# Key products from ScalarE to VectorE, state decay from ScalarE to GpSimd, and two regrouped slots, in a fused attention, FFN and MoE kernel

## Chip, cores and metric

The kernel runs on 1 core of one Trainium2 chip. The metric is the device time of one execution in microseconds (us), the median of several runs. All times here are in us unless marked ns.

## The reference, cut to what matters

Three stages follow each other on 2 x 768 = 1536 tokens of width 512 (8 heads of 64): a linear attention with decay, a dense FFN, and a mixture of experts with one expert per token.

```python
# 1 attention, per batch and head, in blocks, kv_state starts at 0
intra = einsum(einsum(qb, kb) * Dmask, vb)          # Dmask = lam ** (i - j), i >= j
inter = einsum(qb * lam_pow, kv_state)
out   = intra + inter
kv_state = lam_block * kv_state + einsum(kb * rev_pow, vb)
# 2 dense FFN: w_in 512 x 2048, w_out 2048 x 512
h = x @ w_in;  x2 = maximum(0.01 * h, h) @ w_out
# 3 MoE, 8 experts of 512 x 1024 x 512
logits = x2 @ w_gate + modality_bias[modality_id];  e = argmax(logits)
out = softmax(logits)[e] * (maximum(x2 @ w1[e], 0) @ w2[e])
...
```

## The kernel before, in words

The order of all instructions is written by hand: each engine runs its own instructions in the order in which the program emits them, and waits for semaphores of the others where it needs their data or a free buffer. So an instruction that waits holds up everything that was emitted behind it on its engine.

**Attention.** Each batch is cut into 6 chunks of 128 tokens, 12 chunks in all, taken in the order of the list ORD: (0,0), (1,0), (0,1), (1,1), (0,2), (1,2), (0,3), (0,4), (0,5), (1,3), (1,4), (1,5), as (batch, chunk). Chunk n goes through these steps:

- at_scores (L290): 8 TensorE products of keys and queries into two PSUM banks.
- at_prep_q (L276, VectorE): the queries times powers of lam, in place.
- at_mask (L304, VectorE): two products of 128x512, scores times the decay mask.
- at_prep_k (L282): the keys times each head's factor for their token, in place, needed only for the state. Before, it is 8 ScalarE instructions of 128x64 (one per head, L288), often emitted in two halves of 4 heads.
- at_out (L317): 8 to 16 products into one bank (masked scores times values, then state times queries), and xt_split (L341), which rounds the result on ScalarE (xh, L349) and takes the rest on VectorE (xl, L350). Chunks 4 and 5 are first copied by ScalarE (L337) and split later.
- at_state (L352): 8 small products of keys and values, and the decay of the state tile in place. Before, the decay is 4 ScalarE instructions of 128x128 (L368) for each chunk whose number within its batch is 1 to 4.
- at_state_add (L372): VectorE adds the products to the state (two instructions of 64x256, L382).

**FFN.** Two chunks make a token block j of 256 tokens (j = 0 to 5). The hidden width 2048 is cut into 16 slices f. A unit is u = 16 j + f, 96 in all. The main loop (L1499) runs iterations i over a list seq of units: blocks 0 and 1 are interleaved (0, 1, 2, 16, 3, 17, ...), from u = 32 on they are in order. One iteration emits ff1 of its unit (12 TensorE products of 128x256 into one of two banks, ScalarE's scaled copy t, L399), ff1_max (VectorE, L404), ff1_split (ScalarE gh, L411; VectorE gl, L412), then ff2 of the unit two iterations earlier (6 products of 128x512, L425), and then the hooks of its unit: attention and routing steps that a table `at(j, f, fn, ...)` has put there. In block j, slot f means unit 16 j + f.

In iterations 0 to 25 the dense weights are also converted from 64-bit floats: three VectorE bit operations per weight slice (L1485, L1490), ScalarE's rounding (L1495), VectorE's remainder (L1497). One slice has 512 KB, and one to two slices are done per iteration.

**Routing.** When block r is through the FFN, evac_x2 (L445) copies its two banks to tiles x2s, of which there is one pair, on ScalarE (L451) and VectorE (L453), and stores them to DRAM. route_dot is 16 VectorE dot products of 128x512 (8 experts, 2 tiles, L503), two per unit. route_v1 (VectorE) picks the expert, route_rk (TensorE, L535 to L539) ranks the tokens with small products, route_v2 and route_gate follow; route_gate stores the gate column of x2s to DRAM.

**Towards the experts.** In the last block (j = 5) the first expert's weights are loaded and split into a rounded part (ScalarE, L865) and a remainder (VectorE, L866): first_w1(i) and first_w2(i) for i = 0 to 3, placed in slots of that block. early_idx, first_gather and TX(0) prepare the first gathered tokens. Then come the expert products G1 and G2.

The slots that the change touches:

```python
SLOT = {2: (None, 2, 5, 7, 10, 10, 12, 13, 15)}   # others: (5, 6, 8, 8, 11, 10, 12, 13, 13)
s_ld, s_a, s_o, s_s, s_d, s_a2, s_o2, s_s2, s_d2 = ...
# load, first(n), out(n), state(n), add(n), first(n+1), out(n+1), state(n+1), add(n+1)
at(2, 10, lambda: evac_x2(1))      # banks 3, 4, where chunk 7's scores go (sb = 3, 4)
RSLOT = {..., 4: (82, 1, 89, 90)}  # first dot unit, experts per unit, route_v1, route_rk
```

Of the kernel before, what the change touches and what calls it, by code (L numbers as in the profile page):

```python
# [12 lines left out]
AF = mybir.ActivationFunctionType  # L13
# [7 lines left out]
E, FE = 8, 1024  # L21
# [18 lines left out]
def tile_attention_ffn_moe(  # L40
# [241 lines left out]
    def at_prep_k(n, heads=range(H)):  # L282
        b, c = ORD[n]
        t = chunks[n]
        if c + 1 >= NCH:
            return
        for h in heads:
            nc.scalar.activation(out=t["k"][:, h, :], in_=t["k"][:, h, :], func=AF.Copy, scale=dec[:, h, C - 1:C])  # L288
# [63 lines left out]
    def at_state(n, bk):  # L352
# [13 lines left out]
        if c > 0:  # L366
            for g in range(4):
                nc.scalar.activation(  # L368
                    out=state[b][:, g, :], in_=state[b][:, g, :], func=AF.Copy, scale=lq[:, g, C - 1:C]
                )  # L370
# [946 lines left out]
    at_mask_tw(1)  # L1317
    at_out(0, 3)
    at_out(1, 4)
    at_prep_k(0)  # L1320
    at_prep_k(1)
    conv("wi", 1, win, V)
# [41 lines left out]
    def xt_staged(n):  # L1364
# [3 lines left out]
    at(0, 7, at_prep_k, 4, range(H // 2))  # L1368
    at(0, 8, at_prep_k, 4, range(H // 2, H))
# [5 lines left out]
    at(0, 11, at_prep_k, 5, range(H // 2))  # L1375
    at(0, 12, at_prep_k, 5, range(H // 2, H))
# [13 lines left out]
        2: (None, 2, 5, 7, 10, 10, 12, 13, 15),  # L1390
    }
    for j in range(2, last):
        n = 2 * (j + 1)
        sb = (5, 6) if j % 2 else (3, 4)
        s_ld, s_a, s_o, s_s, s_d, s_a2, s_o2, s_s2, s_d2 = SLOT.get(j, (5, 6, 8, 8, 11, 10, 12, 13, 13))
# [4 lines left out]
        at(j, s_a, at_prep_k, n, range(H // 2))  # L1400
        at(j, s_a + 1, at_prep_k, n, range(H // 2, H))
# [3 lines left out]
        at(j, s_s, at_prep_k, n + 1, range(H // 2))  # L1405
        at(j, s_s + 1, at_prep_k, n + 1, range(H // 2, H))
# [7 lines left out]
    RSLOT = {0: (32, 1, 39, 41), 1: (42, 1, 49, 51), 2: (52, 1, 59, 61), 3: (66, 1, 73, 75), 4: (82, 1, 89, 90)}  # L1414
    for r, (f0, step, fv, fr) in RSLOT.items():
        for i in range(0, E, step):
            jobs = [(e, tk) for e in range(i, i + step) for tk in range(2)]
            at(0, f0 + i // step, route_dot, r, jobs)
        at(0, fv, route_v1, r)
        at(0, fr, route_rk, r, 7)  # L1420
        at(0, fr, route_v2, r)
        at(0, fr, route_pf, r)
        at(0, fr, route_gate, r)
# [29 lines left out]
    at(last, 11, early_idx)  # L1453
    at(last, 12, first_gather)
    at(last, 15, TX, 0)
    for i in range(4):
        at(last, (3, 13, 14, 15)[i], first_w1, i)
        at(last, (6, 8, 10, 12)[i], first_w2, i)
# [230 lines left out]
```

## Time and profile before

| | us |
|---|---|
| median of 3 runs (lowest, highest) | 534.59 (531.89, 535.84) |
| profiled execution, its device time | 532.42 |
| its span from first to last instruction | 530.5 |
| mean granted TensorE clock, share of full speed | 0.980 |

Busy in that span: TensorE (PE) 499.1 us, 94%; VectorE (DVE) 316.2, 60%; ScalarE (ACT) 194.8, 37%; GpSimd (POOL) 49.7, 9%. PE is busy for nearly all of the span, so the rest is in few places: what counts is where PE stands idle, which engine it then waits for, and how fast its clock is afterwards. A share over the whole span says little about an engine in one stage.

### The profile page before, as it was taken

What the parts mean: (1) busy time and instruction counts of PE and PEld (TensorE: products, weight loads), DVE (VectorE), ACT (ScalarE), POOL (GpSimd) and SP (SyncE); (2) the same over time, 40 slices, a digit from 0 to 9 for tenths busy, and PEclk for the clock granted to TensorE, in tenths of its full rate; (3) what the DMA queues carried; (4) which work ended last, traced back from release to release, by engine and by line L of the source; (5) the groups of instructions that cost most, each with busy time, mean ns of one, the idle gap of its engine ahead of it and who ended that gap; (6) DMA issues with size and microseconds to landing.
All of it is one profiled execution on the core that took longest, in us unless ns stands there. A gap on an engine that the chain in (4) does not pass through costs nothing. (4 is left out here: it accounts for less than half of the span.)

```text
span 530.5 us, 9446 instructions
## 1 busy us (share of the span) xinstructions
PE 499.1 (94%) x3485; PEld 425.7 (80%) x3485; DVE 316.2 (60%) x796; ACT 194.8 (37%) x489; POOL 49.7 (9%) x97
## 2 busy tenths in 40 slices
PE   5868999999999799999999999899999999999994
PEld 3757988686988689788988889787789987879693
DVE  5696998887577467667477647874551251513130
ACT  2456345454433332333333334354222253322221
POOL 1000000002000000000000000020140302322111
PEclk9988999999999899999999999989999999999998
DMA  8999201701801100410050008211069608274101
GB/s 257 359 407 401 103 1 34 260 2 45 278 1 41 40 2 1 139 41 1 21 138 22 2 20 279 61 42 40 7 215 400 219 22 312 78 245 157 41 2 42
DMA packets 30669, 63.43 MB, mean 120 GB/s; under 512 B 6871, under 2 KB 8799, under 8 KB 30608
## 3 DMA queue, kind: packets, MB, share of 16 engines
q1 hardware_dynamic: 28496, 56.17, 30.8%
q0 software_dynamic: 2112, 6.52, 3.6%
q8 instruction: 29, 0.48, 0.4%
q14 instruction: 32, 0.26, 0.2%
HBM read 56.35 MB, written 6.52 MB: 119 GB/s over the span
## 5 line engine op out<-in xcount | busy, mean ns | idle before, releaser
L396 PE MATMUL hp<-xh,wi 128*128 128x256 f32 x768 | 128.5, 290 | 4.9 <-ACT xh L349 2.7
L425 PE MATMUL x<-wo,gh 128*128 128x512 f32 x384 | 122.8, 402 | 1.7 <-DVE pm L309 1.7
L396 PEld LDWEIGHTS hp<-xh,wi 128*128 128x128 f32 x768 | 110.6, 194 | 14.2 <-DVE t L404 4.7
L425 PE MATMUL x<-wo,gl 128*128 128x512 f32 x192 | 76.6, 399 | 0.1
L425 PEld LDWEIGHTS x<-wo,gh 128*128 128x128 f32 x384 | 67.4, 194 | 10.2 <-issue 1.9
L411 ACT ACTIVATE gh<-t 128x256 fp32r<-128x256 f32 x96 | 40.1, 418 | 81.9 <-DVE t L404 81.9
L396 PE MATMUL hp<-xl,wi 128*128 128x256 f32 x384 | 62.5, 285 | 0.0
L404 DVE TENSOR_TENSOR t<-t,hp 128x256 f32<-128x256 f32 x96 | 40.2, 419 | 34.2 <-ACT t L399 32.9
L412 DVE TENSOR_TENSOR gl<-t,gh 128x256 fp32r<-128x256 f32 x96 | 40.7, 424 | 33.4 <-ACT gh L411 26.1
L399 ACT ACTIVATE t<-hp 128x256 f32<-128x256 f32 x96 | 36.2, 377 | 63.6 <-PE hp L396 63.2
L954 PE MATMUL hp<-xp,w1h 128*128 128x256 f32 x320 | 58.7, 284 | 0.0
L396 PEld LDWEIGHTS hp<-xl,wi 128*128 128x128 f32 x384 | 53.5, 193 | 0.4 <-DVE xl L350 0.4
L982 PE MATMUL o<-w2h,hp 128*128 128x512 f32 x160 | 52.5, 397 | 0.0
L954 PEld LDWEIGHTS hp<-xp,w1h 128*128 128x128 f32 x320 | 50.2, 192 | 2.6 <-issue 2.5
L964 DVE SCALAR_TENSOR_TENSOR hp<-hp,hp 128x256 fp32r<-128x256 f32 x40 | 16.5, 423 | 60.0 <-ACT hp L963 27.8
L425 PEld LDWEIGHTS x<-wo,gl 128*128 128x128 f32 x192 | 36.8, 192 | 11.8 <-DVE gl L412 3.6
L954 PE MATMUL hp<-xp,w1l 128*128 128x256 f32 x160 | 45.3, 283 | 0.0
L982 PEld LDWEIGHTS o<-w2h,hp 128*128 128x128 f32 x160 | 29.8, 188 | 7.0 <-issue 1.2
L982 PE MATMUL o<-w2l,hp 128*128 128x512 f32 x80 | 31.5, 393 | 0.0
L954 PEld LDWEIGHTS hp<-xp,w1l 128*128 128x128 f32 x160 | 30.7, 192 | 0.1
L963 ACT ACTIVATE hp<-hp 128x256 fp32r<-128x256 f32 x40 | 15.2, 384 | 41.2 <-PE hp L954 40.9
L503 DVE SCALAR_TENSOR_TENSOR junk<-x2s,wgr_hi 128x512 bf16<-128x512 f32 x40 | 27.5, 689 | 0.7
(248 smaller groups left out, 625.9 us busy)
## 6 DMA issues: line engine op xcount, KB each, us to landing
rawi<-in_moe_w_in_dram SPq DMA_DIRECT2D x16, 512.0 KB, 7.9
rawo<-in_moe_w_out_dram SPq DMA_DIRECT2D x16, 512.0 KB, 7.4
raw<-in_moe_w_dram SPq DMA_DIRECT2D x16, 512.0 KB, 3.9
nr<-in_moe_w_dram SPq DMA_DIRECT2D x9, 512.0 KB, 12.3
xs_d<-x2s SPq DMA_DIRECT2D x12, 256.0 KB, 4.4
nrx<-in_moe_w_dram SPq DMA_DIRECT2D x6, 512.0 KB
wgr_hi<-in_moe_w_dram SPq DMA_DIRECT2D x6, 512.0 KB, 8.6
qT<-in_q_dram SPq DMA_DIRECT2D x10, 256.0 KB, 6.7
```

What stands on the lines that cost most here:

```text
L396: nc.tensor.matmul(hp, lhsT=w[:, hl, kk, :], rhs=xx[:, kk, :], start=(n == 0), stop=(n == 11))
L399: nc.scalar.activation(out=t, in_=hp, func=AF.Copy, scale=0.01)
L404: nc.vector.tensor_max(out=t, in0=t, in1=hp)
L411: nc.scalar.activation(out=gh, in_=t, func=AF.Copy)
L412: nc.vector.tensor_sub(out=gl, in0=t, in1=gh.bitcast(F32))
L425: nc.tensor.matmul(x2[j][tk], lhsT=a[:, ts], rhs=wout[f][:, w, :], start=(f == 0 and n == 0), stop=(f == 15 and n == 2),)
L503: nc.vector.scalar_tensor_tensor(out=junk, in0=x2s[j][tk][:, 0:512], scalar=1.0, in1=wgr[e], op0=ALU.mult, op1=ALU.mult, accum_out=lgs[j][ ...
L954: nc.tensor.matmul(hp.rearrange("p (a b) -> p a b", a=2), lhsT=w1s[kk][w][:, f * 128:(f + 1) * 128], rhs=x[:, :, ks], start=(n == 0), stop ...
L963: nc.scalar.activation(out=hi, in_=hp, func=AF.Relu)
L964: nc.vector.scalar_tensor_tensor(out=lo, in0=hp, scalar=0.0, in1=hi.bitcast(F32), op0=ALU.max, op1=ALU.subtract)
L982: nc.tensor.matmul(o2[b], lhsT=hT[b, f // 4][a][fs], rhs=w[:, f % 2, :], start=(n == 0), stop=(n == 23))
```

## The change

- at_prep_k is one VectorE product of 128x512, with the factor of each head repeated by a zero step, in place of 8 ScalarE instructions. Where it was emitted in two halves, it stands where the second half stood (chunks 4, 5, 6, 8, 10) or one unit before the chunk's at_state (chunks 7 and 9).
- The decay of the state is two GpSimd products of 64x256 (the diagonal blocks; the rest of the tile is zero), in place of 4 ScalarE instructions of 128x128.
- Before the main loop, the bit operations of the second weight slice are emitted ahead of the first two at_out, and its rounding behind them.
- In block 2 the second chunk (7) moves two units later: scores, query and mask from slot 10 to 12, out from 12 to 14, state from 13 to 15; the state add of chunk 6 moves from 10 to 9. In blocks 3 and 4 the first chunk's state (with the load of the next chunk's v and k) moves from slot 8 to 9, the second chunk's state add from 13 to 14.
- Block 4's dot products are three per unit (units 82 to 87) in place of two; route_v1 moves from unit 89 to 87, route_rk, route_v2 and route_gate from 90 to 89.
- early_idx moves from unit 91 to 90; first_w1(0) from unit 83 to 88; first_w2(0 to 3) from units 86, 88, 90, 92 to 88, 89, 91, 92.

```diff
-    def at_prep_k(n, heads=range(H)):
+    def at_prep_k(n):
         b, c = ORD[n]
         t = chunks[n]
-        if c + 1 >= NCH:
-            return
-        for h in heads:
-            nc.scalar.activation(out=t["k"][:, h, :], in_=t["k"][:, h, :], func=AF.Copy, scale=dec[:, h, C - 1:C])
+        if c + 1 < NCH:
+            nc.vector.tensor_tensor(
+                out=t["k"], in0=t["k"], in1=dec[:, :, C - 1:C].to_broadcast([128, H, D]), op=ALU.mult
+            )
...
-            for g in range(4):
-                nc.scalar.activation(
-                    out=state[b][:, g, :], in_=state[b][:, g, :], func=AF.Copy, scale=lq[:, g, C - 1:C]
+            for half in range(2):
+                p0 = half * 64
+                sl = state[b][p0:p0 + 64, :, p0:p0 + 64]
+                nc.gpsimd.tensor_tensor(
+                    out=sl, in0=sl, in1=lq[p0:p0 + 64, :, C - 1:C].to_broadcast([64, 4, 64]), op=ALU.mult
                 )
...
+    first = split64([("wi", 1, win, V)])
     at_out(0, 3)
     at_out(1, 4)
+    split64_out(*first)
     at_prep_k(0)
     at_prep_k(1)
-    conv("wi", 1, win, V)
...
-    at(0, 7, at_prep_k, 4, range(H // 2))
-    at(0, 8, at_prep_k, 4, range(H // 2, H))
+    at(0, 8, at_prep_k, 4)
...
-    at(0, 11, at_prep_k, 5, range(H // 2))
-    at(0, 12, at_prep_k, 5, range(H // 2, H))
+    at(0, 12, at_prep_k, 5)
...
-        2: (None, 2, 5, 7, 10, 10, 12, 13, 15),
+        2: (None, 2, 5, 7, 9, 12, 14, 15, 15),
...
-        s_ld, s_a, s_o, s_s, s_d, s_a2, s_o2, s_s2, s_d2 = SLOT.get(j, (5, 6, 8, 8, 11, 10, 12, 13, 13))
+        s_ld, s_a, s_o, s_s, s_d, s_a2, s_o2, s_s2, s_d2 = SLOT.get(j, (5, 6, 8, 9, 11, 10, 12, 13, 14))
...
-        at(j, s_a, at_prep_k, n, range(H // 2))
-        at(j, s_a + 1, at_prep_k, n, range(H // 2, H))
+        at(j, s_a + 1, at_prep_k, n)
...
-        at(j, s_s, at_prep_k, n + 1, range(H // 2))
-        at(j, s_s + 1, at_prep_k, n + 1, range(H // 2, H))
+        at(j, s_s2 - 1, at_prep_k, n + 1)
...
-    RSLOT = {0: (32, 1, 39, 41), 1: (42, 1, 49, 51), 2: (52, 1, 59, 61), 3: (66, 1, 73, 75), 4: (82, 1, 89, 90)}
+    RSLOT = {0: (32, 2, 39, 41), 1: (42, 2, 49, 51), 2: (52, 2, 59, 61), 3: (66, 2, 73, 75), 4: (82, 3, 87, 89)}
...
-    at(last, 11, early_idx)
+    at(last, 10, early_idx)
...
-        at(last, (3, 13, 14, 15)[i], first_w1, i)
-        at(last, (6, 8, 10, 12)[i], first_w2, i)
+        at(last, (8, 13, 14, 15)[i], first_w1, i)
+        at(last, (8, 9, 11, 12)[i], first_w2, i)
```

## Rows read from the trace of the kernel before

**Rows 1.** Windows: busy us and instruction counts of each engine, granted clock, DMA.

```profile
25.00:45.00 20.00, 12.87 (x111) 10.72 (x111) 17.95 (x35) 12.38 (x36) 0.00 (x0) 0.91 1.03 405
56.00:128.00 72.00, 69.07 (x479) 57.09 (x477) 61.84 (x128) 33.19 (x86) 3.17 (x8) 1.00 0.19 62
182.00:188.00 6.00, 6.00 (x31) 5.49 (x31) 4.53 (x11) 0.38 (x1) 0.00 (x0) 0.50 0.23 87
189.00:340.00 151.00, 149.72 (x1088) 132.64 (x1087) 102.17 (x289) 52.75 (x142) 3.88 (x21) 1.00 0.21 64
345.00:348.00 3.00, 3.00 (x12) 2.61 (x11) 2.54 (x10) 1.89 (x6) 0.67 (x2) 0.51 0.03 3
```

**Rows 2.** Timeline (start, duration, instruction, idle before and releaser): two FFN units.

```profile
335.88 0.64 PE L396 MATMUL hp<-xh,wi 128*128 128x256 f32 x4
...
338.70 0.64 PE L396 MATMUL hp<-xh,wi 128*128 128x256 f32 x4
```

**Rows 3.** Timeline, the conversion stage around chunk 4's state decay.

```profile
95.62 1.26 ACT L368 ACTIVATE st<-st,lq 128x128 f32<-128x128 f32 x4
...
97.19 0.42 DVE L404 TENSOR_TENSOR t<-t,hp 128x256 f32<-128x256 f32 x1 [1.46 <-ACT t L399]
...
97.66 0.74 PE L396 MATMUL hp<-xh,wi 128*128 128x256 f32 x4 [1.03 <-DVE t L404]
...
100.39 0.42 DVE L404 TENSOR_TENSOR t<-t,hp 128x256 f32<-128x256 f32 x1 [0.30 <-ACT t L399]
```

**Rows 4.** Timeline, the conversion stage around chunk 4's key products.

```profile
87.80 1.05 ACT L288 ACTIVATE k<-k,dec_t 128x64 f32<-128x64 f32 x4
...
88.75 0.57 ACT L337 COPY kT<-ao 128x512 f32<-128x512 f32 x1
...
89.63 0.42 DVE L404 TENSOR_TENSOR t<-t,hp 128x256 f32<-128x256 f32 x1 [1.73 <-ACT t L399]
```

**Rows 5.** Timeline, the start: a weight load, its first use, a decay, the split.

```profile
15.39 0.33 SPq L163 DMA_DIRECT2D rawi<-in_moe_w_in_dram  x1
...
23.96 0.42 DVE L1485 TENSOR_SCALAR tw<-rawi 128x512 int32<-128x512 int32 x1
...
41.46 1.26 ACT L368 ACTIVATE st<-st,lq 128x128 f32<-128x128 f32 x4
...
43.24 0.69 DVE L350 TENSOR_TENSOR xl<-ao,xh 128x512 fp32r<-128x512 f32 x1 [2.01 <-ACT xh L349]
```

**Rows 6.** The page's DMA issues: count, size of one, median us to landing.

```profile
rawi<-in_moe_w_in_dram SPq DMA_DIRECT2D x16, 512.0 KB, 7.9
```

**Rows 7.** Timeline, the scores of chunk 7 and the copy before them.

```profile
181.04 0.59 ACT L451 COPY x2s<-x 128x512 f32<-128x512 f32 x1 [0.67 <-DMA xs_d<-x2s]
...
181.68 2.67 PE L296 MATMUL sc<-qT,kT 64*128 64x128 f32 x16 [3.34 <-ACT x2s L451]
```

**Rows 8.** Timeline, block 4's rank products and VectorE's queue around them.

```profile
343.83 0.41 DVE L404 TENSOR_TENSOR t<-t,hp 128x256 f32<-128x256 f32 x1
...
343.97 0.17 PE L535 MATMUL rk<-oh,tri_b 128*128 128x8 bf16 x1 [2.28 <-DVE oh L527]
...
359.81 0.41 DVE L404 TENSOR_TENSOR t<-t,hp 128x256 f32<-128x256 f32 x1
```

**Rows 9.** Groups by form: count, busy us, mean ns of one, idle before.

```profile
L280 DVE TENSOR_TENSOR qT<-qT,lq 128x512 f32<-128x512 f32 x8 | 5.5, 689 | 3.9 <-PE sc L296 3.9
L865 ACT ACTIVATE w1h<-raw 128x1024 fp32r<-128x1024 f32 x8 | 8.1, 1049 | 0.9 <-DMA raw<-in_moe_w_dram 0.5 <-ACT hp L963 0.4
L619 POOL TENSOR_TENSOR mmat<-mmat,nst 128x64 f32<-128x64 f32 x1 | 0.3, 297 | 0.1
L1263 POOL TENSOR_SCALAR nh<-nh,xgn 32x512 f32<-32x512 f32 x3 | 4.7, 1571 | 24.1 <-DVE nh L1262 24.1
```

**Rows 10.** Timeline, VectorE beside GpSimd's only other stretch of products.

```profile
123.51 0.70 POOL L239 CAST tri_b<-tri_f 128x128 bf16<-128x128 f32 x1 [121.14 <-DMA tri_f<-in_tri_dram]
...
123.97 0.78 DVE L1497 TENSOR_TENSOR wo<-tw,wo 128x512 fp32r<-128x512 f32 x1
```

More of the change, by code (lines that the diff above doesn't have):

```diff
@@ L1411, in tile_attention_ffn_moe @@
         at(j, s_d2, at_state_add, n + 1)
-    RSLOT = {0: (32, 1, 39, 41), 1: (42, 1, 49, 51), 2: (52, 1, 59, 61), 3: (66, 1, 73, 75), 4: (82, 1, 89, 90)}
[L1415 to L1418, printed above, removed]
+    RSLOT = {0: (32, 2, 39, 41), 1: (42, 2, 49, 51), 2: (52, 2, 59, 61), 3: (66, 2, 73, 75), 4: (82, 3, 87, 89)}
+    for r, (f0, n, fv, fr) in RSLOT.items():
+        jobs = [(e, tk) for e in range(E) for tk in range(2)]
+        for i in range(0, len(jobs), n):
+            at(0, f0 + i // n, route_dot, r, jobs[i:i + n])
         at(0, fv, route_v1, r)
```

## Prediction

> **What bounds the kernel now.** I read the windows by stage first, then the waits of PE, then the timeline around each. In the windows the reader is to see that PE is busy in nearly every microsecond from unit 26 on (149.72 of 151.00 us between 189 and 340) at the full 2.4 GHz, and that the earlier stages differ: between 25 and 45 us PE does 12.87 of 20.00 us while VectorE does 17.95, and between 56 and 128 us PE does 69.07 of 72.00 with VectorE at 61.84 [rows 1]. A unit that waits for nothing takes 2.82 us on PE [rows 2].
>
> In the conversion stage (iterations 4 to 25) a unit takes longer, because a loop through two engines sets the pace: VectorE's last bit operation lets ScalarE round the weight, ScalarE's copy t queues behind that rounding, and VectorE's next ff1_max waits for t. It repeats every 3.20 us (97.19 to 100.39), and VectorE waits 0.30 us in it [rows 3]. PE has 0.38 us to spare per unit, so there whatever ScalarE does between the rounding and t is on the path. From unit 26 on PE sets the pace, with two stalls that count: 3.34 us ahead of chunk 7's scores, which wait for ScalarE's copy of the bank [rows 7], and 2.28 us ahead of block 4's rank products [rows 8]. After each, PE's granted clock is at 1.2 GHz for some time: 0.50 over the whole of 182 to 188 us, 0.51 over 345 to 348 [rows 1].
>
> **The start (to iteration 4).** ScalarE's key products of chunks 0 and 1 go, so t of unit 0 comes earlier. VectorE then meets the next wait: the third weight slice. Its load is issued at 15.39 and such a load lands 7.9 us later in the median, at 23.3 us; VectorE first reads it at 23.96 without waiting [rows 5, 6]. So 0.7 us is gained (0 if it landed just before the read), and the new key products of chunks 0 and 1 on VectorE sit in the wait for that load. From there VectorE is never idle until it waits 2.01 us for chunk 3's rounding, which stands behind chunk 2's decay of 1.26 us on ScalarE [rows 5]. Chunk 2's key product adds 0.69 us to VectorE's run (the nearest row is the query product of the same shape, 689 ns [rows 9]). Sum: 0.7 - 0.69 + 1.26 = 1.3 us. Chunk 3's decay stands between rounding and t as in the next part and gives another 1.2 if PE is not then late itself; PE is at the lower clock for part of this stretch (0.91 mean [rows 1]), so half of it is likely. I take -2.0, bounds 0 and -3.5. The bit operations of the second slice move ahead of the first two splits; they fill time in which VectorE waits for the first output, and cost at most their own length of about 1.8 us if that slice landed late, which the wait for the third slice would still cover.
>
> **The conversion stage.** Chunks 4 and 5 each lose two things from the loop. The decay: VectorE waits 1.46 us for t in place of 0.30, so 1.16 us, and PE stalls 1.03 us for it [rows 3]. The second half of the key products: the copy behind them starts at 88.75 in place of 87.80, so 0.95 us; VectorE waits 1.73 us there, which leaves room for its new 0.69 us instruction [rows 4, 9]. The first halves (unit 7 and 11) stand beside VectorE's masks and are worth nothing. Sum 2 x (1.16 + 0.95) = 4.2 us. PE's own work is next late: it needs 2.82 of the 3.20 us, so a unit without attention work catches up by 0.38, and in one with outputs or scores PE is the later one and what VectorE saved there shows only some units on. With ten such units to catch up in, nearly all of it arrives. I take -4.2, bounds -2.5 and -4.5.
>
> **GpSimd's decay.** No row shows 64x256. A product of 128x64 took 297 ns, one by a scalar of 32x512 1571 [rows 9]; between them 256 columns are 0.84 us, a pair 1.7, against 1.26 on ScalarE. Nothing queues behind it that is due: the pair can start as soon as at_out has read the state, while the add comes one to four units (2.82 us each) later. The tightest is chunk 7, state and add both at unit 47, output at 46: 1.7 us against at least one unit. If an op took over 2 us, VectorE would wait there and PE behind it by the excess. The other cost is VectorE beside GpSimd. In the one place where they overlap closely a 128x512 subtraction took 0.78 us beside a cast, against 0.69 [rows 10, 9]. A pair overlaps some three VectorE instructions: 0.3 us. It counts for chunks 2 to 5, where VectorE or the loop sets the pace: 1.2 us; later VectorE has slack (102.17 of 151 us [rows 1]). Bounds 0 and the full 4 x 1.7 = 6.8.
>
> The Trainium skill (SBUF — State Buffer, Who interferes with whom) speaks against this edit: the port is an exclusive lock, and a VectorE instruction with two SBUF inputs contends with a GpSimd instruction that reads SBUF, so that the later one "fully blocks". The 0.09 us of rows 10, in an instruction that was covered by the cast for half of its time, does not agree with a full block, but the cast has one input. By the rule the upper bound above would be the price.
>
> **Scores two units later.** The copy at 181.04 waits for the store of the gate column, the end of a chain that started with block 0's rank products; the scores want its bank [rows 7]. Emitted at unit 44, they leave PE two units (5.6 us) of work that needs neither, and the copy takes 0.59 us on ScalarE, its twin on VectorE about as long as any 128x512 there (0.69 [rows 9]). The chain itself gets shorter too, since ScalarE's key products of chunk 7, which waited there for their load, move to VectorE at unit 46. So the 3.34 us go, and with them the slow clock: 182 to 188 us at 0.50 is 3 us lost [rows 1]. Together -6.4 us. What could be late next: chunk 7's output at unit 46 is now due for ff1 of unit 48, one unit and a state product later, some 3.5 us for a rounding and a subtraction of 0.7 each; VectorE's queue (scores, query, mask and two dots in unit 44) runs late by less than the one unit that the second hp bank allows. Nothing, then; bound: half of the 6.4 back. The loads of v and k that move a unit in blocks 3 and 4 are still three units (8.5 us) ahead of their use, and SP has no store queued behind them in those units; state and adds there have the same cover. Nothing.
>
> **The last rank.** The stall of 2.28 us and the slow clock (3 us at half: 1.5 lost, with its edges near 1.9) would give 4.2 us [rows 8, 1]. I don't count them. VectorE's queue is what is late: the rank waits behind route_v1, that behind the dots, and after the rank products the same queue still runs late: from 343.83 to 359.81 five ff1_max, 3.20 us a unit against PE's 2.82 [rows 8, 2]. Dots, expert picks, index work and weight splits from unit 82 to 95 are the same in number before and after; only their order changes. So the last ff1_max of the block can't come earlier than the sum of the work lets it, and PE will wait for ff1_max of units 89 and 90, about 1 us each, where it waited for the rank. One thing is lost: the splits at units 83 to 88 had ScalarE's half (1.05 us [rows 9]) beside VectorE's dots; at unit 88 there are no dots left, and VectorE waits for it, 0.7 us (1.05 less the third of a us in which ff1_split runs beside it). I take +0.5; bounds -4.2 and +1.0.
>
> **Sum.** -2.0 - 4.2 + 1.2 - 6.4 + 0.5 = -10.9 us. Against the profiled execution (532.42, span 530.5) that is 521.5; it lay 2.2 us under the median of the runs, from which it would be 523.7. I predict 523.
>
> **Rivals.** (1) *The rank's stall pays in full*: if VectorE's queue has more slack at units 88 to 95 than I count, 4.7 us more: 518. For it: PE is 94% busy overall and its stall is real; against: the pace of rows 8. (2) *The gap of chunk 7 moves*: the later output makes unit 48 wait, or the copy is still late; the stall or the slow clock comes back by half, 526. Against: VectorE's and ScalarE's low load there (4.53 and 0.38 of 6 us [rows 1]). (3) *The start gives nothing*: the third slice lands at 23.9 and the key products lengthen VectorE's run: 525. (4) *The lock*: GpSimd's pairs block VectorE for their whole time in chunks 2 to 5: 6.8 in place of 1.2, 529. The price is GpSimd's from rows 9; the mechanism is the one that the Trainium skill states (SBUF — State Buffer, Who interferes with whom). (5) *Slower*: the same blocking with a dear decay. At the price of 32x512, 1.57 us an op, four pairs cost 12.6 us, and the whole gain before contention (12.1) is gone: that is the point from which it decides. At 2.3 us an op (two inputs, one repeated) it would be 18.4 and the time 540. Against: 297 ns at 64 columns. (6) That the change doesn't do what it says would be a rank or scores that still stall where they stood; that is within (2).
>
> **How the numbers follow.** Forecast 0.50, (1) 0.17, (2) 0.13, (3) 0.08, (4) 0.08, (5) 0.04. From (1) with the start at its better bound some 516, from (4) 529; so 516 to 528.5 leaves out (5), part of (4) and a little below. A measurement of this kernel can tell about 1% (5.3 us) from no change: faster by more has the forecast, (1), (3), most of (2) and half of (4), 0.89; within 1% the rest of (2) and (4), 0.07; slower 0.04.
>
> **What would show it.** In the profile after: no ScalarE instructions at the lines of key products and decay; ten VectorE products near 0.69 us and sixteen GpSimd ones near 0.84; in the conversion stage no wait of VectorE for t above 0.8 us, and PE's stall of 1.03 gone; PE without a stall and at full clock where chunk 7's scores stood; no wait for the rank, but PE waiting for ff1_max around units 91 and 92. The prediction is wrong if GpSimd's products stretch VectorE's beyond 0.1 us each, if a stall with a slow clock reappears between units 42 and 52, or if the stretch from unit 82 to the expert products gets shorter by more than 1 us.

## The result and the profile after

| | before | after |
|---|---|---|
| median of 4 runs (lowest, highest) | 533.77 (531.89, 535.84) | 518.39 (517.50, 519.68) |
| ratio, 95% interval | | 0.9713 (0.9668 to 0.9757) |
| profiled execution, device time | 532.42 | 519.68 |
| its span | 530.5 | 517.9 |
| mean granted TensorE clock | 0.980 | 0.988 |

The change makes the kernel 15.4 us faster by the medians; 523 was predicted, with 516 to 528.5 as range. Between the spans of the two profiled executions the difference is 12.6 us; the profiled one of after was the longest of its four, that of before lay under its median.

Where it came from is read by one mark that both traces have 96 times, the start of ff1_max on VectorE. Its start before less its start after is the gain up to that iteration:

| iteration | before | after | gain | stage behind it |
|---|---|---|---|---|
| 4 | 50.99 | 47.15 | 3.84 | start |
| 14 | 85.00 | 81.17 | 3.83 | conversion, no attention work |
| 26 | 130.69 | 123.53 | 7.16 | conversion with chunks 4 and 5 |
| 38 | 165.62 | 158.48 | 7.14 | |
| 49 | 208.52 | 194.56 | 13.96 | gap ahead of chunk 7's scores |
| 81 | 315.43 | 301.19 | 14.24 | |
| 95 | 359.81 | 346.21 | 13.60 | last rank |
| end of span | 530.5 | 517.9 | 12.6 | experts |

The lines of after that answer to those of before (its line numbers are 2 higher from L370 on, and 1 lower in the main loop's conversion). First the windows by stage, in the columns of [rows 1]: the start, the conversion, the place of chunk 7's scores, the rest up to the last rank, the first expert products.

```profile
25.00:45.00 20.00, 15.97 (x134) 13.46 (x133) 19.06 (x38) 7.88 (x17) 4.02 (x4) 0.83 1.03 405
52.00:121.00 69.00, 68.24 (x481) 57.64 (x480) 64.25 (x131) 27.29 (x62) 7.23 (x13) 1.00 0.24 82
174.00:180.00 6.00, 6.00 (x49) 5.21 (x48) 5.00 (x13) 1.55 (x4) 0.00 (x0) 1.00 0.16 62
180.00:326.00 146.00, 145.04 (x1061) 127.98 (x1060) 101.88 (x294) 42.58 (x109) 8.92 (x30) 1.00 0.21 66
347.00:351.00 4.00, 3.39 (x8) 2.46 (x9) 2.34 (x3) 1.50 (x3) 0.00 (x0) 0.63 0.00 0
```

Where chunk 7's scores stood at half clock before, the third window is now at full clock. VectorE's share of the start has risen to 19.06 of 20 us, ScalarE's fallen to 7.88. A new place with a low clock, 0.63, stands at 347.

The groups of the two moved operations (count, busy us, mean ns of one, idle before):

```profile
L370 POOL TENSOR_TENSOR st<-st,lq 64x256 f32<-64x256 f32 x16 | 13.4, 836 | 208.6 <-PE ao L335 177.8 <-ACT wi L1494 30.2
L286 DVE TENSOR_TENSOR k<-k,dec_t 128x512 f32<-128x512 f32 x7 | 5.2, 745 | 0.0
L286 DVE TENSOR_TENSOR kv<-kv,dec_t 128x512 f32<-128x512 f32 x3 | 2.0, 681 | 0.0
```

Sixteen decay products at 836 ns, as estimated (0.84 us), but by luck, since the mean mixes undisturbed products with ones that wait: the line's own view gives 616 ns at the least, 624 in the median and 1852 at the most. The timeline of the conversion stage shows when longer ones occur, at chunk 4's pair (GpSimd's rows first, then VectorE's; the last row is the wait at iteration 17):

```profile
80.10 1.25 POOL L370 TENSOR_TENSOR st<-st,lq 64x256 f32<-64x256 f32 x1 [38.98 <-PE ao L335]
81.43 0.62 POOL L370 TENSOR_TENSOR st<-st,lq 64x256 f32<-64x256 f32 x1
...
80.12 0.42 DVE L414 TENSOR_TENSOR gl<-t,gh 128x256 fp32r<-128x256 f32 x1
...
81.51 1.09 DVE L1489 SCALAR_TENSOR_TENSOR tw<-rawi,tw 128x512 int32<-128x512 int32 x1
...
83.13 0.68 DVE L1489 SCALAR_TENSOR_TENSOR tw<-rawi,tw 128x512 int32<-128x512 int32 x1
...
91.66 0.42 DVE L406 TENSOR_TENSOR t<-t,hp 128x256 f32<-128x256 f32 x1 [0.29 <-ACT t L401]
```

The bit operation that began 0.08 us after GpSimd's second product took 1.09 us; the same instruction alone takes 0.68. That is what the pair costs VectorE, 0.4 us, and it is above the 0.1 us that the prediction gave as a sign of being wrong. The pair starts three iterations before the place where ScalarE did the decay. There, at iteration 17, VectorE's wait for t is now 0.29, where it was 1.46 [rows 3].

The start, in the timeline as in [rows 5]:

```profile
22.08 0.43 DVE L1484 TENSOR_SCALAR tw<-rawi 128x512 int32<-128x512 int32 x1 [0.87 <-DMA rawi<-in_moe_w_in_dram]
...
32.43 1.85 POOL L370 TENSOR_TENSOR st<-st,lq 64x256 f32<-64x256 f32 x1 [30.21 <-ACT wi L1494]
...
32.52 0.68 DVE L1496 TENSOR_TENSOR wi<-tw,wi 128x512 fp32r<-128x512 f32 x1
33.12 0.68 DVE L280 TENSOR_TENSOR qk<-qk,lq 128x512 f32<-128x512 f32 x1
...
40.79 0.69 DVE L350 TENSOR_TENSOR xl<-ao,xh 128x512 fp32r<-128x512 f32 x1 [0.85 <-ACT xh L349]
```

The third slice's load is now waited for, 0.87 us; the wait for chunk 3's rounding has fallen from 2.01 to 0.85. Chunk 2's first decay product takes 1.85 us here, while VectorE's two instructions beside it keep their 0.68: at this place it is GpSimd that waits. The timeline at chunk 7's scores, as in [rows 7]:

```profile
172.12 0.59 ACT L453 COPY x2s<-x 128x512 f32<-128x512 f32 x1 [0.68 <-DMA xs_d<-x2s]
...
176.57 0.38 PE L296 MATMUL sc<-qT,kT 64*128 64x128 f32 x2
```

The copy is done at 172.71 and the scores come at 176.57 without a wait. The timeline of the last rank, as in [rows 8], and of the first expert products behind it:

```profile
324.46 0.18 PE L537 MATMUL rk<-oh,tri_b 128*128 128x8 bf16 x1
...
328.30 0.73 PE L398 MATMUL hp<-xh,wi 128*128 128x256 f32 x4 [0.64 <-DVE t L406]
...
332.02 0.74 PE L398 MATMUL hp<-xh,wi 128*128 128x256 f32 x4 [0.66 <-DVE t L406]
...
345.06 1.23 DVE L868 TENSOR_TENSOR w1l<-raw,w1h 128x1024 fp32r<-128x1024 f32 x1 [0.52 <-ACT w1h L867]
...
346.21 0.41 DVE L406 TENSOR_TENSOR t<-t,hp 128x256 f32<-128x256 f32 x1
...
347.61 0.50 PE L921 MATMUL h<-w1h,xgh 128*128 128x512 f32 x1 [1.81 <-ACT xgh L907]
```

PE no longer waits for the rank. It waits for ff1_max twice (0.64 and 0.66) and then 1.81 us for the first gathered tokens, whose rounding stands on ScalarE behind gh, which waits for the last ff1_max, which stands on VectorE behind a weight split. The stall has moved 23 us down the program, and the lower clock with it.

### The profile page after: what moved, and what is told of

It reads as the page before. It is cut to its first block, busy times and chain, and to the rows that moved or that the text cites. A ratio compares the mean times of both kernels' runs of the same rounds, so it can differ in the third digit from the quotient of the medians.

```text
span 517.9 us, 9366 instructions
## 1 busy us (share of the span) xinstructions
PE 494.3 (95%) x3485; PEld 421.7 (81%) x3485; DVE 323.0 (62%) x806; ACT 166.4 (32%) x377; POOL 62.5 (12%) x113
## 5 line engine op out<-in xcount | busy, mean ns | idle before, releaser
L398 PE MATMUL hp<-xh,wi 128*128 128x256 f32 x768 | 127.1, 288 | 3.4 <-ACT xh L349 2.1
L427 PE MATMUL x<-wo,gh 128*128 128x512 f32 x384 | 121.2, 397 | 0.6 <-DVE pm L309 0.6
L398 PEld LDWEIGHTS hp<-xh,wi 128*128 128x128 f32 x768 | 109.2, 191 | 12.4 <-DVE t L406 3.6
L427 PE MATMUL x<-wo,gl 128*128 128x512 f32 x192 | 75.5, 393 | 0.0
L427 PEld LDWEIGHTS x<-wo,gh 128*128 128x128 f32 x384 | 66.3, 191 | 9.2 <-PE hp L398 0.8
L370 POOL TENSOR_TENSOR st<-st,lq 64x256 f32<-64x256 f32 x16 | 13.4, 836 | 208.6 <-PE ao L335 177.8
```

Of the source, the lines that this page charges most:

```text
L370: nc.gpsimd.tensor_tensor(out=sl, in0=sl, in1=lq[p0:p0 + 64, :, C - 1:C].to_broadcast([64, 4, 64]), op=ALU.mult)
L398: nc.tensor.matmul(hp, lhsT=w[:, hl, kk, :], rhs=xx[:, kk, :], start=(n == 0), stop=(n == 11))
L427: nc.tensor.matmul(x2[j][tk], lhsT=a[:, ts], rhs=wout[f][:, w, :], start=(f == 0 and n == 0), stop=(f == 15 and n == 2),)
```

## The experiments

Each time below is the median of its runs; the ratio is to the kernel before on the same chip. The runs were on several chips, on which the median of the kernel before lay between 531.67 and 533.77, so differences of about 2 us between the times below are read by the ratios and traces. The 95% interval of the changed kernel is 0.9668 to 0.9757. Gains and losses by iteration are read at ff1_max, as above.

### slots_back: block 2's slots as before

```diff
-        2: (None, 2, 5, 7, 9, 12, 14, 15, 15),
+        2: (None, 2, 5, 7, 10, 10, 12, 13, 15),
```

> The changed kernel with block 2 as it was: chunk 7's scores at unit 42, its output at 44, its state at 45, chunk 6's state add at 42 (the key product of chunk 7 comes along to unit 44). Theory (the gap in front of the scores is the store of the gate column plus the slow clock behind it, and the two units of work cover it): PE waits again some 3 us for ScalarE's copy, granted clock near 0.5 for some 6 us behind it, and the time is 6 to 7 us over the changed kernel's 518.4, so 524 to 525.5. Rival (the chain to the store got shorter because ScalarE's key products of chunk 7 are gone from it, and this did most): the wait is under 1.5 us, no slow clock behind it, and the time is at most 521.

523.21 (519.92 to 525.65), ratio 0.981 (0.9757 to 0.9863). The scores wait again, in the timeline:

```profile
173.93 0.59 ACT L453 COPY x2s<-x 128x512 f32<-128x512 f32 x1 [0.67 <-DMA xs_d<-x2s]
...
174.56 1.75 PE L296 MATMUL sc<-qT,kT 64*128 64x128 f32 x16 [1.30 <-ACT x2s L453]
```

and in its windows, of the six us from there on:

```profile
174.00:180.00 6.00, 5.33 (x32) 4.73 (x33) 5.04 (x11) 0.90 (x2) 0.18 (x2) 0.73 0.23 87
```

1.30 us in place of 3.34 [rows 7], and a clock of 0.73 over six us where it was 0.50 [rows 1]. Between iterations 38 and 49 it loses 3.5 us to the changed kernel (2.26 to 5.79), not 6.8. So neither theory holds alone: some half of the gap had gone already without the new slots, but half of it stays.

### before_slots: the new slots alone

The same line changed in the kernel before, in the other direction.

> The kernel before with one line changed: block 2's slots as in the changed kernel (chunk 7's scores at unit 44, output at 46, state at 47, chunk 6's add at 41). Key products and decay stay on ScalarE, in halves at units 39 and 40 for chunk 7. Theory (the 7 us between iterations 38 and 49 are two stalls in a row: ScalarE's key products of chunk 7 wait 3.17 us for their load with the copy t behind them, and the scores wait for the copy of the bank; each part of the change removes one): the first stays, the second goes, 3 to 4 us faster than before. Rival, the prediction as it stood (the stall of the scores and its slow clock are all of it): 6 to 7 us faster.

529.55 over 10 runs, ratio 0.9943 (0.9917 to 0.9968): 3.0 us faster. The scores come without a wait, but VectorE is held up ahead of them, in the timeline:

```profile
173.46 1.07 ACT L288 ACTIVATE k<-k,dec_t 128x64 f32<-128x64 f32 x4 [3.37 <-DMA k<-in_k_dram]
...
174.83 0.42 DVE L404 TENSOR_TENSOR t<-t,hp 128x256 f32<-128x256 f32 x1 [2.80 <-ACT t L399]
...
183.95 1.16 PE L296 MATMUL sc<-qT,kT 64*128 64x128 f32 x16
```

ScalarE stands 3.37 us at chunk 7's key products, whose load has not landed, with the copy t of an FFN unit behind them; the kernel before has the same wait with 3.17 us. Iterations 38 to 49 gain 4.1 us here (0.15 to 4.23), and slots_back, which has the key products on VectorE but not the slots, gains 3.3 over before in the same stretch (4.88 to 8.17). Together that is 7.4, against 6.8 in the changed kernel. Two stalls in a row, each removed by another part of the change. For the first, the place counts and not the engine: in keys_scalar (below) ScalarE does the same products at unit 46, without a wait for the load, and the stretch from iteration 38 to 49 loses only 0.9.

### rank_back: the last rank as before

```diff
-    RSLOT = {..., 4: (82, 3, 87, 89)}
+    RSLOT = {..., 4: (82, 2, 89, 90)}
...
-    at(last, 10, early_idx)
+    at(last, 11, early_idx)
-        at(last, (8, 13, 14, 15)[i], first_w1, i)
-        at(last, (8, 9, 11, 12)[i], first_w2, i)
+        at(last, (3, 13, 14, 15)[i], first_w1, i)
+        at(last, (6, 8, 10, 12)[i], first_w2, i)
```

> The changed kernel with the last rank as it was: two dots per unit, route_v1 at unit 89, the rank at 90, index work at 91, weight splits at units 83, 86, 88, 90, 92. Theory (VectorE's work from unit 82 to the first expert products sets the end, and where PE waits in between does not matter): PE waits over 2 us for the rank again with a granted clock near 0.5 behind it, the waits for ff1_max of units 91 and 92 (0.64 and 0.66) and the 1.81 for the first gathered tokens shrink, and the time is within 1.5 us of the changed kernel, 517 to 519. Rival (the rank's stall pays in full): 4 us slower, 522.5.

518.73 (517.64 to 521.0), ratio 0.974 (0.9698 to 0.9781): the same time. PE waits 2.3 us for the rank again, and the wait for the first tokens is gone. From iteration 81 to 95 this kernel is 0.72 us quicker than the changed one (3.34 to 2.62). That is the first half of the theory; rank_back_late below has the other.

### late_splits: two weight splits out of VectorE's queue

```diff
-        at(last, (8, 9, 11, 12)[i], first_w2, i)
+        if i < 2:
+            at(last, (8, 9)[i], first_w2, i)
+    at(last, 15, first_w2, 2)
+    at(last, 15, first_w2, 3)
```

> The changed kernel with the splits of w2's third and fourth parts moved from units 91 and 92 to unit 95, behind the first gathered tokens and the last split of w1. Theory (VectorE's queue from unit 82 on sets when the expert products start; two splits of 1.23 us stand in it that are needed only 12 us later, and VectorE is idle for 2.84 us ahead of the last evacuation): the wait of 1.81 for the rounded tokens and the slow clock behind it go, 2 to 3.5 us faster than the changed kernel, 515 to 516.5. Rival (the wait is for the tokens' path itself: transposition, ScalarE's queue): under 0.5 us gained, or lost again at the evacuation or where the second product waits for w2.

516.02 (515.14 to 517.04), ratio 0.9698 (0.9673 to 0.9723). From iteration 81 to 95 it gains 2.82 us on the changed kernel, in iterations 92 and 93, where the splits stood, and the expert products start without a wait for the tokens, in the timeline:

```profile
342.59 0.41 DVE L406 TENSOR_TENSOR t<-t,hp 128x256 f32<-128x256 f32 x1
...
343.59 0.60 ACT L907 ACTIVATE xgh<-gt 128x512 fp32r<-128x512 f32 x1
...
344.79 0.39 PE L921 MATMUL h<-w1h,xgh 128*128 128x512 f32 x1
```

The windows behind it:

```profile
346.00:349.00 3.00, 3.00 (x17) 2.48 (x15) 3.00 (x4) 1.62 (x3) 0.00 (x0) 1.00 0.09 36
```

The clock stays at 1.00 behind them. The medians differ by 2.4 us, but its interval lies within that of the changed kernel, so it is the traces that show the gain.

### rank_back_late: the old rank with the late splits

rank_back and late_splits together: the rank at unit 90, w2's last two splits at unit 95.

> The changed kernel with the last rank as before (two dots per unit, the rank at unit 90, first split of w1 at 83, of w2 at 86 and 88), and with w2's third and fourth split at unit 95 as in late_splits. Theory (once two splits are out of VectorE's queue, the rank's own stall is what is left, so here the two units pay): PE waits about 2.3 us for the rank with a granted clock near 0.5 behind it, not all made up behind it, 1.5 to 4 us slower than late_splits, 517.5 to 520. Rival (the order of the rank never matters, only the sum of VectorE's work): within 0.7 us of late_splits, 515.5 to 516.7.

517.92 (515.85 to 522.54), ratio 0.972 (0.9689 to 0.9751), 1.9 us over late_splits, with intervals that overlap. The rank in its timeline, and VectorE's wait for t three units behind it:

```profile
334.07 0.17 PE L537 MATMUL rk<-oh,tri_b 128*128 128x8 bf16 x1 [2.28 <-DVE oh L529]
...
343.88 0.42 DVE L406 TENSOR_TENSOR t<-t,hp 128x256 f32<-128x256 f32 x1 [1.57 <-ACT t L401]
```

and the window behind it:

```profile
334.00:337.00 3.00, 2.93 (x18) 2.93 (x18) 2.09 (x11) 1.10 (x5) 1.29 (x4) 0.53 0.00 0
```

From iteration 81 to 95 it gains 0.69 us on the changed kernel, as rank_back does without the late splits (0.72), where late_splits gains 2.82. With the old rank the stall and the clock behind it (0.53) set the end of the block and the splits are free; with the new rank the splits set it. Each hides the other: starting from rank_back, the new order alone gives nothing (-0.72) and the late splits alone give nothing (-0.03), and both together give 2.1 us.

### decay_scalar: the decay back on ScalarE

The 4 ScalarE instructions of 128x128 of the kernel before, in place of the two GpSimd products.

> The changed kernel with the state decay as 4 ScalarE instructions of 128x128 per chunk, key products on VectorE. Theory: the conversion iterations behind chunks 4 and 5 lose 1.16 each again, less the 0.4 that VectorE's two-input bit operation loses beside GpSimd; at the start VectorE waits again some 2 us for chunk 3's rounding behind the decay of chunk 2. Together 3 to 4 us slower than the changed kernel, 521.5 to 522.5. Rival (GpSimd's contention eats the decay's gain): within 1 us, 518 to 519.5.

524.47 (523.32 to 525.53), ratio 0.9847 (0.9806 to 0.9888). Iterations 17 and 25 lose 1.16 and 1.17 against the changed kernel, iterations 15 and 23 win 0.41 and 0.40 back, where the pair on GpSimd had stretched a bit operation; both terms are the expected ones. Iteration 4 loses 1.17, and VectorE's wait for chunk 3's rounding is 2.01 again. Up to iteration 38 that makes 2.8 us, just under the range that was expected. From iteration 54 to 57, in block 3, come 4.1 us more, since this trace's scores of chunk 8 waited 2.8 us for their load (early_load, below), and 1.5 come back in the expert stage; its span is 5.9 us longer than that of the changed kernel. The medians are 6.1 us apart; that the other three runs had the same wait is not shown.

### keys_scalar: the key products back on ScalarE

8 ScalarE instructions of 128x64 at the place of each VectorE product.

> The changed kernel with each chunk's key products as 8 ScalarE instructions of 128x64, all at the place where the changed kernel has its one VectorE product, decay on GpSimd. Theory: the conversion iterations behind chunks 4 and 5 lose 0.5 to 0.95 each, more since the 8 now stand together (2.1 us in ScalarE's queue ahead of the copy t): up to 2 us each; the start loses 0.7 to 1.5. Together 2.5 to 5 us slower than the changed kernel, 521 to 523.5. Rival (what the start gained is the order of the bit operations, and the loop has room for ScalarE's keys once the decay is gone): within 1 us.

525.62 (525.37 to 526.04), ratio 0.9878 (0.9838 to 0.9917), 7 us slower than the changed kernel and outside both ranges. ScalarE's queue behind chunk 4's output, in the timeline:

```profile
85.10 2.01 ACT L287 ACTIVATE k<-k,dec_t 128x64 f32<-128x64 f32 x8
87.01 0.56 ACT L336 COPY kT<-ao 128x512 f32<-128x512 f32 x1
87.47 0.38 ACT L400 ACTIVATE t<-hp 128x256 f32<-128x256 f32 x1
...
87.88 0.42 DVE L405 TENSOR_TENSOR t<-t,hp 128x256 f32<-128x256 f32 x1 [2.69 <-ACT t L400]
```

Iterations 15 and 23 lose 1.89 each, the start 0.73, chunk 7's unit 0.94: 5.45 of the 5.7 us that this trace has at iteration 95. Eight together cost more than the two halves of before did, since all 2.01 us stand ahead of t.

### order_back: the second slice's bit operations behind the first outputs

```diff
-    first = split64([("wi", 1, win, V)])
     at_out(0, 3)
     at_out(1, 4)
-    split64_out(*first)
     at_prep_k(0)
     at_prep_k(1)
+    conv("wi", 1, win, V)
```

> The changed kernel with the second weight slice converted as before: its bit operations, rounding and remainder all behind the first two at_out. Theory (VectorE is bound at the start by the landing of the third slice and by its own length, so an order that only fills a wait is worth little): 0 to 1 us slower than the changed kernel, and VectorE waits over 1 us for the first outputs' rounding (1.50 and 0.83 before, 0.59 after). Rival (the order gave most of the start's 3.8 us): 2 to 3.5 us slower. The start itself came out 2.36 us apart in two traces with the same code in it, so only the waits named and the first ff1_max decide, less the total.

521.44 (519.77 to 524.83), ratio 0.9819 (0.9781 to 0.9858): slower, by 3 us of the medians, which is the rival's range. The waits for the first outputs' rounding are back at 1.49 and 0.57. VectorE's first read of the third slice, in the timeline:

```profile
23.28 0.42 DVE L1483 TENSOR_SCALAR tw<-rawi 128x512 int32<-128x512 int32 x1
```

It comes without a wait, at 23.28 against 22.08 behind a wait of 0.87 in the changed kernel. So with the old order VectorE's own run is late, and not the load, and the 1.2 us between the two are still there at iteration 4. But the profiled execution is its shortest, with a span of 518.0, and 1.2 us lies inside the spread of the changed start itself: seven traces with that start reach iteration 4 between 46.17 and 49.51. So the order is worth something; how much over all executions, one trace can't say.

### decay_twice: the contention by itself

```diff
                     out=sl, in0=sl, in1=lq[p0:p0 + 64, :, C - 1:C].to_broadcast([64, 4, 64]), op=ALU.mult
                 )
+            for half in range(2 if n < 6 else 0):
+                ...
+                nc.gpsimd.tensor_tensor(out=sc2, in0=sc2, in1=..., op=ALU.mult)   # sc2: 64x256 of a scratch tile
```

> The changed kernel with a second pair of 64x256 products behind each decay pair of chunks 2 to 5 on GpSimd, on a scratch tile that nobody waits for (the result is the same). Theory (a pair costs VectorE 0.4 us where it overlaps a two-input bit operation, and nothing waits for GpSimd): 0.4 to 0.5 in each of iterations 17 and 25, 0.3 to 0.6 twice at the start, together 1.5 to 2 us slower. Rival (an exclusive lock for the whole length of GpSimd's products): 1.7 per pair, 6.8 us slower. Second rival (the add waits for GpSimd's queue): VectorE shows waits for GpSimd at the adds.

522.5 (520.13 to 523.09), ratio 0.9823 (0.9796 to 0.985). In the trace iterations 15 and 23 lose 0.84 and 0.85, the start nothing (-0.05); 1.65 in all, more than expected since not one but three of VectorE's instructions are hit, and no wait of VectorE for GpSimd is seen. The medians lie 4.1 us apart, more than the profiled execution shows; that part has no row. The timeline of the two added products of chunk 4 and of VectorE beside them (GpSimd's rows first):

```profile
82.07 0.95 POOL L376 TENSOR_TENSOR junk<-junk,lq 64x256 f32<-64x256 f32 x1
83.10 0.96 POOL L376 TENSOR_TENSOR junk<-junk,lq 64x256 f32<-64x256 f32 x1
...
81.46 1.08 DVE L1495 SCALAR_TENSOR_TENSOR tw<-rawi,tw 128x512 int32<-128x512 int32 x1
...
82.47 1.11 DVE L1502 TENSOR_TENSOR wo<-tw,wo 128x512 fp32r<-128x512 f32 x1
83.50 1.11 DVE L1495 SCALAR_TENSOR_TENSOR tw<-rawi,tw 128x512 int32<-128x512 int32 x1
```

Here both engines take turns: VectorE's instructions last 1.08 to 1.11 in place of 0.68, GpSimd's 0.95 in place of 0.62. Each extension, 0.33 to 0.43, is a little under the time that was left of the other engine's instruction when this one began (0.47 to 0.56). At the start they don't: GpSimd's first product of chunk 2 took 2.37 us in this trace, from 31.73 on, and VectorE's three instructions beside it 0.69 each, which fits that the start loses nothing.

### decay_vector: the decay on VectorE

`nc.gpsimd` to `nc.vector` in the two decay products.

> The changed kernel with the same two decay products of 64x256 on VectorE in place of GpSimd. No product of that shape on VectorE stands in a trace, but the state's add of 64x256 does; at 0.4 us each a pair adds 0.8 to VectorE's queue. Theory (GpSimd's pair costs the conversion stage about 0.4 by contention and VectorE's own pair would cost 0.8): 0.4 slower in each of iterations 15 to 17 and 23 to 25, 0.3 to 0.8 twice at the start, together 1 to 2 us slower, 519.5 to 520.5. Rival (contention with GpSimd is the dearer): same or faster, 517.5 to 518.5.

521.23 (520.54 to 522.37), ratio 0.9789 (0.9751 to 0.9827). The conversion stage loses only 0.46 us (1.18 at iteration 14, 1.64 at 38): what VectorE's own pair costs at iterations 17 and 25 it wins for the most part back at 15 and 23, 0.41 each, where no GpSimd product stands beside it. The rest of this trace's 1.7 at iteration 95 is the start, again inside its spread. So GpSimd is better than VectorE for the decay by little.

### early_load and both: the loads of chunk 8

```diff
-SLOT.get(j, (5, 6, 8, 9, 11, 10, 12, 13, 14))
+SLOT.get(j, (2 if j == 3 else 5, 6, 8, 9, 11, 10, 12, 13, 14))
```

> The changed kernel with the loads of chunks 8 and 9 emitted at unit 50 in place of 53, so ahead of the gate store and of the evacuation's stores in SP's queue. Theory (chunk 8's scores at unit 54 wait for a load issued 3 to 4 us before, for between 0 and 2.8 us by the run, and a slow clock follows): no wait of these scores for a DMA, full clock from 200 to 225 us, and 1 to 3 us faster than the changed kernel with a smaller spread, 515.5 to 517.5. Rival (the load waits for its buffer or lands in time anyway): no difference, 518.4.

517.39 (516.21 to 518.36), ratio 0.9719 (0.9693 to 0.9744): no difference that the ratios show, and the spread of 2.2 us is no smaller than the changed kernel's. The traces do show one. In rank_back, whose attention is that of the changed kernel, the load is issued behind the stores and lands late; in early_load it is long there. The timeline of rank_back:

```profile
206.83 0.45 SPq L153 DMA_DIRECT2D kT<-in_kt_dram  x1
...
212.02 2.04 PE L296 MATMUL sc<-qT,kT 64*128 64x128 f32 x16 [2.30 <-DMA kT<-in_kt_dram]
```

its window behind:

```profile
212.00:216.00 4.00, 3.98 (x27) 3.78 (x28) 1.91 (x4) 0.00 (x0) 0.00 (x0) 0.57 0.02 9
```

and the timeline of early_load, whose load is issued 13 us ahead of the stores:

```profile
190.40 0.42 SPq L153 DMA_DIRECT2D kT<-in_kt_dram  x1
...
203.21 0.80 SPq L562 DMA_DIRECT2D xs_d<-x2s  x2
...
209.60 0.60 PE L296 MATMUL sc<-qT,kT 64*128 64x128 f32 x6
```

Between iterations 54 and 57 early_load gains 1.0 us on the changed kernel's trace, and rank_back loses 2.9 there, decay_scalar 4.1, rank_back_late 4.6, in none of which block 3 was touched but for decay_scalar's decay. So this one load, issued some 4 us ahead of its use, makes up to 4.6 us of difference between executions that issue it late, and 5.6 against early_load.

With the late splits as well:

> late_splits and early_load together: w2's last two splits at unit 95, loads of chunks 8 and 9 at unit 50. Theory (two separate stalls, 3.6 at the end of block 5 and 1.0 or more at unit 54): their gains add, 514 to 515.5, spread under 3 us. Rival (what one gains the other had already): as late_splits, 516.

515.53 (515.27 to 516.05), ratio 0.9682 (0.9652 to 0.9713). It is the fastest kernel here, 2.9 us under the changed one by the medians, and its five runs lie within 0.8 us. Its trace has both gains (1.0 at iterations 54 to 57, 2.82 at 81 to 95). Against late_splits the medians differ by 0.5, which the intervals don't tell apart. Every run of it is under every run of the changed kernel, though the two weren't timed on the same chip, and the intervals of their ratios overlap (0.9652 to 0.9713 and 0.9668 to 0.9757).

## Why the prediction was right, and where it was off

**The start: mis-sized.** Predicted -2.0, with bounds 0 and -3.5; the profiled pair shows 3.84, outside them. The waits are the ones described: VectorE then waits for the third slice, and the decay of chunk 2 goes from behind its wait for chunk 3's rounding. The term that was put too low is the order of the bit operations, said to cost or give little. Without it (order_back) VectorE reads the third slice at 23.28, 0.68 ahead of before, which is the predicted 0.7, and by iteration 2 the gain is 0.09 where 0.0 was worked out. With it VectorE is free for the slice at 21.21, waits, and reads it at 22.08, and the gain by iteration 2 is 1.28. That also took a load that was issued 0.6 us earlier (14.78) and was there after 7.3 us, not 7.9. The decay of chunk 2 gives 1.39 (predicted 1.26), that of chunk 3 1.17 (1.2, of which half was counted). Over all traces the start is less sure than one pair looks: two with the old start reach iteration 4 at 50.86 and 50.99, seven with the new one between 46.17 and 49.51, with 47.62 in the middle. That makes 3.3, and single executions from 1.4 to 4.8.

**The conversion stage and GpSimd's contention: right in sum, the second for another reason.** The decay gives 1.16 and 1.17, as predicted. The key products give 0.53 in each of iterations 15 and 23 where 0.95 was predicted; in decay_scalar, without GpSimd's pair beside them, they give 0.40 more. So 0.4 per pair is the contention, 0.8 for chunks 4 and 5, and nothing measurable at the start (decay_twice), where GpSimd waits instead. Gain 4.2 less 0.8 is 3.4, and 3.33 is what the table shows. The prediction had 3.0 for the two terms, but it spread 0.3 over three instructions from the cast of [rows 10]; here one instruction takes all of it. By the prediction's own sign, a stretch beyond 0.1 us, that step was wrong.

The Trainium skill (SBUF — State Buffer, Who interferes with whom) calls the shared port an exclusive lock, for which a VectorE instruction with two SBUF inputs contends with GpSimd's reads; the words "fully blocks" it uses of VectorE's two-port modes. Such a lock is nearer to the traces than the 0.09 us that was taken from [rows 10]: the bit operation took 1.09 us beside GpSimd's product and 0.68 alone. Nor do [rows 10] speak against it: of the cast only 0.24 us were left when the subtraction began, which covers a third of it and not half. What didn't follow was the price in rival (4). VectorE pays at most for the rest of one instruction that was already under way, 0.4 us, and GpSimd waits in its turn, or for longer (1.85 us for chunk 2); the full 1.7 us of a pair was never paid.

**The gap: right in size, wrong in its cause.** Predicted -6.4, measured 6.8. The step that failed is "so the 3.34 us go, and with them the slow clock", as the work of the new slots alone. before_slots and slots_back show two stalls: ScalarE's 3.2 us at the key products of chunk 7, which came ahead in time, and the scores' wait. The prediction named the first as something that shortens the chain and gave it no price; the new slots alone bring 4.1, the rest of the change without them 3.3. That the sum came out is luck. The rival that the gap moves (2) is out: no wait and no low clock from 174 to 180.

**The last rank: right in size, the reason only half.** +0.5 predicted, 0.64 measured up to iteration 95, with PE's waits for ff1_max ahead of units 91 and 92 where they were expected. Rival (1), the stall pays in full, falls with rank_back (the same time with the stall). But "VectorE's queue is what is late" holds for the new order alone: two splits less in it bring 2.82 us there (late_splits). With the old rank the same two splits less change the end of the block by 0.03 (rank_back_late), and VectorE waits for t. So the 3.20 us a unit behind the old rank [rows 8] were not VectorE's pace. They were PE's, which had no wait there and a lower mean clock (16 us at 0.89 is 1.8 us lost, and the five units took 1.9 more than five times 2.82), in the window of the kernel before:

```profile
344.00:360.00 16.00, 16.00 (x105) 14.31 (x105) 11.65 (x33) 8.37 (x18) 4.41 (x9) 0.89 0.14 35
```

Two limits lay 0.7 us apart, PE's in the old order and VectorE's in the new one. That they did was luck for the term, and the new order has a value of its own, 2.1 us, once two splits are out of the way.

**The end.** From iteration 95 to the end of the span before takes 170.7 us and after 171.7, a loss of 1.0 that no step foresaw. Most of it is the clock behind the new 1.81 us stall. The first expert product comes 0.8 us sooner behind the last ff1_max (1.4 for 2.2), but from there on before takes 168.5 us and after 170.3. Eight of the 14 traces have that stall. In four (after, slots_back, keys_scalar, decay_vector) a low clock follows and the stretch takes 170.3 to 170.5; in the other four it takes 168.75 to 168.95 at full clock; the six without the stall take 168.4 to 168.7. The timeline of early_load, with the same stall:

```profile
346.98 0.50 PE L921 MATMUL h<-w1h,xgh 128*128 128x512 f32 x1 [1.82 <-ACT xgh L907]
```

and its window behind it, where after has 0.63:

```profile
347.00:351.00 4.00, 4.00 (x16) 3.02 (x17) 2.34 (x3) 1.46 (x2) 0.00 (x0) 1.00 0.00 0
```

Why the clock falls in some executions and not in others stays open.

**Sum.** Terms of -10.9 were predicted, and the profiled pair shows 12.6: start 1.8 more, the gap 0.4 more, conversion with contention 0.3 more, the rank 0.14 less, the end 1.0 less. The rest, about 0.25, is the small steps between the stages. The medians differ by 2.8 us more than the pair; three places that vary between executions of the same code, the start (3.3 us), chunk 8's load (up to 4.6) and the clock at the first expert products (1.5), are large enough for that.

## What to carry to other kernels

Before a stall is priced, look along the queue of the engine that it waits for, and for a second stall just ahead of it: removing either may give half, and an edit with two parts can remove both without its author knowing which did. An edit that "gives nothing" may be covered by the next constraint in the same stretch; undo it once more with that constraint taken away (rank_back and rank_back_late) before it is dropped. And a transfer issued one unit ahead of its use is not a cost that one trace can show: compare it over several.

## What the runs showed that was not expected

GpSimd's product of 64x256 takes 0.62 us when VectorE leaves it alone, so that a pair (1.3 us) costs no more than ScalarE's four decay instructions (1.26); beside VectorE's instructions with two inputs in SBUF it took 0.95 to 2.37. Those of VectorE took 1.08 to 1.11 in place of 0.68 where GpSimd's product was under way first, and kept their 0.68 where it came second. VectorE's instructions of 256 columns beside chunk 4's pair kept their 0.42 us, and there it was GpSimd's product that took longer, 1.25.

A short stall can cost more than its length, but its length doesn't say whether it will. The rank's 2.28 us were followed by a clock of 0.53 over 3 us (1.2 GHz is the lower level), the 2.30 us at chunk 8's scores in rank_back by 0.57 over 4 us, and the 1.81 us at the first expert products by 0.63 over 4. But the same 1.82 us in early_load were followed by 1.00, and so were 2.14 us ahead of chunk 8's scores in keys_scalar and 1.17 in late_splits, while 1.30 us in slots_back were followed by 0.73 over 6 us.
